# A 4-column addition between the exponentials' sums and their reciprocals, on GpSimd or on VectorE as a planner chooses

## Chip, cores and metric

The kernel runs on one core of a Trainium2 chip. The metric is the device time of one execution in microseconds, the median of several; smaller is better.

## The reference

Three blocks follow each other: an attention with a narrow causal window and some global keys, and two gated projections. In short:

```python
def _attn_ref(q, k, v, n_global, n_local):          # (2, 8, 768, 64)
    scores = scale * q @ k.T + bias                  # bias = -slope[h] * distance
    scores = where(keep, scores, -1e9)               # keep: k < 8, or 0 <= q - k < 96
    scores = scores - max(scores)
    a = np.exp(scores)
    a = a / (np.sum(a, axis=-1, keepdims=True) + 1e-09)
    return a @ v

def reference(...):
    x = attn_out.transpose(0, 2, 1, 3).reshape(2, 768, 512)
    x = (sigmoid(conv5(x)) * (x @ w_val)) @ w_out            # causal, per channel
    h = relu(x @ w_in)                                        # 512 -> 1024
    return (h * sigmoid(conv3(h))) @ w_out2                   # 1024 -> 512
```

The `1e-09` that is added to the sum of the exponentials is what the change is about.

## The kernel before

Attention works on 12 tiles (2 batches of 6 times 128 queries). A tile needs only its own and the previous 128 keys (256 columns); the global keys are copied over the first columns of the previous tile's (line 545, GpSimd). For each of two halves (4 heads) of a tile:

- TensorE makes the scores (line 492, PSUM tiles `s`).
- For each head VectorE adds mask and bias and takes the least value (line 503), and ScalarE takes the exponential and its sum (line 508). The sums of 4 heads lie beside each other in `st.t[:, 1]`, 128 rows by 4 columns.
- The *guard* (line 519) adds 1e-9 to these 4 columns, VectorE takes their reciprocal (line 522), and each head's probabilities `p` are multiplied by it: the *normalisation*, on VectorE (line 529), GpSimd (line 532) or ScalarE (line 535).

Then TensorE turns two heads' probabilities at a time (transposes, line 562, into the only PSUM bank `t`), ScalarE (line 566) or VectorE (line 572) copies them to `pts`, TensorE multiplies with the values (line 587, PSUM tile `x`), and a copy (line 604 or 610) puts the tile into `x`.

Beside that the weights are prepared: loads of 512 KB into three buffers `raw`, a conversion to fp32 by ScalarE, GpSimd and VectorE (lines 272 to 282), the product of `w_out` and `w_in` on TensorE (line 337, in 8 parts through two PSUM banks `f`) and its split into a high part by ScalarE (`Wh`, line 244) and a low part by VectorE (`Wl`, line 246). The projections follow per batch and half sequence: first tap (line 700 or 701), further taps on VectorE (line 705), tanh (line 707), and matmuls in three passes of high and low parts (lines 253 to 255).

No order is written by hand. Every piece of work is given to a `Plan` with an engine, an expected duration, and what it reads and writes. `Plan.add` takes one engine (and more as keywords); `Plan.any` takes a table of ways. `lay` builds a list schedule, backward for the ranks and forward for the order, in 6 passes, and `issue` keeps the pass with the earliest expected end. Where a piece has several ways, it goes where it is expected to end first:

```python
def here(w, e):
    ends = {o: max(free[o], est[w]) + us for o, (us, _) in w.ways.items()}
    return back or min(ends, key=ends.get) == e
```

All engines then run their instructions strictly in the planned order, and each waits for what its next instruction needs. So one changed duration or choice can move any work on any engine.

Of the kernel before, what the change touches and what calls it, by code (L numbers as in the profile page):

```python
# [14 lines left out]
ALU = mybir.AluOpType  # L15
# [205 lines left out]
def act_us(n, sbuf=True, scaled=False, sums=False):  # L221
    return 0.05 + 0.000834 * n + 0.042 * sbuf + 0.092 * scaled + 0.093 * sums


def dve_us(n, scaled=False):
    return 0.069 + 0.001042 * n + 0.061 * scaled
# [209 lines left out]
def fast_attention(c, ap):  # L436

    nc, ident, pl = c.nc, c.ident, c.plan
# [13 lines left out]
    def keys(t, pr, what):  # L452
        return key_tile(t)[:, pr, what]
# [18 lines left out]
    def held(d, ts):  # L472
        return [d[t] for t in ts if t in d]

    for t in range(nt):
        b, i = tiles[t]
        if t and i == 0:
            yield
        js = [t - 1, t] if i else [t]
        nk = len(js) * P  # L480
        st, p = sts.new(), {}
        load(t)
        for half in range(2):
            s = [c.ring["s"].new() for z in range(2)]

            def scores(half=half, s=s, js=js, t0=t):
                for pr in (2 * half, 2 * half + 1):
                    for n, j in enumerate(js):
                        for z in range(2):
                            hs = slice(z * D, (z + 1) * D)  # L490
                            out = s[z].t.rearrange("p (a w) -> p a w", w=WIN)[:, pr % 2, n * P : (n + 1) * P]
                            nc.tensor.matmul(out, keys(t0, pr, 1)[hs], keys(j, pr, 0)[hs], start=True, stop=True)  # L492

            pl.add(
                "PE", 0.43 * len(js), scores, s + held(kq, js), [("kq", j) for j in js], [("s", t, half)], mode="s"
            )
            for h in range(4 * half, 4 * half + 4):
                p[h] = pr_.new()

                def least(h=h, s=s, st=st, w=p[h], nk=nk, i=i):  # L500
                    sc = s[h % 2].t.rearrange("p (a w) -> p a w", w=WIN)[:, h // 2 % 2, :nk]
                    bias = c.B[:, h, :] if i else c.B0[h]
                    nc.vector.tensor_tensor_reduce(  # L503
                        w.t[:, :nk], sc, bias, -QKSCALE, 3.0e38, ALU.add, ALU.min, st.t[:, 0, h : h + 1]
                    )

                def grow(h=h, st=st, w=p[h], nk=nk):
                    nc.scalar.activation(  # L508
                        w.t[:, :nk], w.t[:, :nk], AF.Exp, bias=st.t[:, 0, h : h + 1], scale=-1.0,
                        accum_out=st.t[:, 1, h : h + 1],  # L510
                    )

                bias = ("B" if i else "B0", h)
                pl.add("DVE", dve_us(nk), least, [p[h], s[h % 2], st], [("s", t, half), bias], [("p", t, h)])
                pl.add("ACT", act_us(nk, True, True, True), grow, [p[h], st], [], [("p", t, h)])
            hs = slice(4 * half, 4 * half + 4)

            def guard(st=st, hs=hs):
                nc.gpsimd.tensor_scalar(st.t[:, 1, hs], st.t[:, 1, hs], 1.0e-9, 1.0, ALU.add, ALU.mult)

            def invert(st=st, hs=hs):
                nc.vector.reciprocal(st.t[:, 2, hs], st.t[:, 1, hs])  # L522

            four = [("p", t, h) for h in range(4 * half, 4 * half + 4)]
            pl.add("POOL", 0.12, guard, [st], four, [("r", t, half)])
            pl.add("DVE", 0.2, invert, [st], [], [("r", t, half)])
            for h in range(4 * half, 4 * half + 4):
                def on_dve(h=h, st=st, w=p[h], nk=nk):
                    nc.vector.tensor_scalar(w.t[:, :nk], w.t[:, :nk], st.t[:, 2, h : h + 1], None, ALU.mult)

                def on_pool(h=h, st=st, w=p[h], nk=nk):
                    nc.gpsimd.tensor_scalar(w.t[:, :nk], w.t[:, :nk], st.t[:, 2, h : h + 1], 1.0, ALU.mult, ALU.mult)  # L532

                def on_act(h=h, st=st, w=p[h], nk=nk):
                    nc.scalar.activation(w.t[:, :nk], w.t[:, :nk], AF.Copy, scale=st.t[:, 2, h : h + 1])

                pl.add(
                    "DVE", 0.22 + 0.00052 * nk, on_dve, [p[h], st], [("r", t, half)], [("p", t, h)],
                    POOL=(0.2 + pool_us(nk), on_pool), ACT=(act_us(nk, True, True), on_act),
                )  # L540

        def first_keys(t=t, i=i):
            r = key_tile(t)[:, :, 0, 0:GW]
            a, z = (gl, r) if i == 0 else (r, gl)
            nc.gpsimd.tensor_scalar(a, z, 1.0, 1.0, ALU.mult, ALU.mult)

        if i == 0:
            pl.add("POOL", 0.4, first_keys, held(kq, [t]), [("kq", t)], ["gl"])
        elif i < NT - 1:
            pl.add("POOL", 0.4, first_keys, held(kq, [t]), ["gl"], [("kq", t)])  # L550

        xp = c.ring["x"].new()
        pts = {}
        for pr in range(NPAIR):
            pt = c.ring["t"].new()
            pts[pr] = ptr.new()

            def turn(pr=pr, pt=pt, p=p, nw=len(js)):
                o = pt.t.rearrange("p (z n q) -> p z n q", z=2, n=2)
                for z in range(2):  # L560
                    for n in range(nw):
                        nc.tensor.transpose(o[:, z, n, :], p[2 * pr + z].t[:, n * P : (n + 1) * P], ident)  # L562

            def copy(pt=pt, w=pts[pr], nw=len(js)):
                o = pt.t.rearrange("p (z n q) -> p z n q", z=2, n=2)
                nc.scalar.activation(w.t[:, :, :nw, :], o[:, :, :nw, :], AF.Copy)  # L566

            two = [p[2 * pr], p[2 * pr + 1]]
            pl.add("PE", 0.218 * len(js), turn, [pt] + two, [("p", t, 2 * pr), ("p", t, 2 * pr + 1)], [("pt", t, pr)])
            def by_dve(pt=pt, w=pts[pr], nw=len(js)):  # L570
                o = pt.t.rearrange("p (z n q) -> p z n q", z=2, n=2)
                nc.vector.tensor_copy(w.t[:, :, :nw, :], o[:, :, :nw, :])

            pl.add(
                "ACT", act_us(2 * nk, False), copy, [pt, pts[pr]], [("pt", t, pr)], [("pts", t, pr)],
                DVE=(dve_us(2 * nk), by_dve),
            )

            if pr % XPAIRS < XPAIRS - 1:
                continue  # L580

            def output(prs=range(pr - XPAIRS + 1, pr + 1), pts=pts, xp=xp, js=js):
                o = xp.t.rearrange("p (a q) -> p a q", q=P)
                for pr in prs:
                    for n, j in enumerate(js):
                        for z in range(2):
                            nc.tensor.matmul(  # L587
                                o[z * D : (z + 1) * D, pr, :], vals(j, 2 * pr + z), pts[pr].t[:, z, n, :],
                                start=n == 0, stop=n == len(js) - 1,
                            )  # L590

            prs = range(pr - XPAIRS + 1, pr + 1)
            pl.add(
                "PE", 0.213 * len(js) * XPAIRS, output, [xp] + [pts[q] for q in prs] + held(vs, js),
                [("pts", t, q) for q in prs] + [("v", j) for j in js], [("xp", t, q) for q in prs], mode="x",
            )
        if 0 < i < NT - 1:
            pl.add(
                "SP", dma_us(64), lambda b=b, t=t: nc.sync.dma_start(vs[t].t[0:GW], c.v[b, 0:GW].rearrange("s (a h) d -> s a h d", a=2)),
                [vs[t]], [], [("v", t)], delay=LANDING,  # L600
            )
        pl.add(
            "ACT", act_us(512, False),
            lambda xp=xp, i=i: nc.scalar.activation(
                c.x[:, :, XP + i * P : XP + (i + 1) * P], xp.t.rearrange("p (a q) -> p a q", q=P), AF.Copy
            ),
            [xp], [("xp", t, pr) for pr in range(NPAIR)], [("x", i)] + (["d", "d0"] if t in (0, 1, 4) else []),
            DVE=(
                dve_us(512),
                lambda xp=xp, i=i: nc.vector.tensor_copy(  # L610
                    c.x[:, :, XP + i * P : XP + (i + 1) * P], xp.t.rearrange("p (a q) -> p a q", q=P)
                ),
            ),
        )
# [431 lines left out]
```

## Time and profile before

| | us |
|---|---|
| median of 3 runs | 285.17 (284.56 to 285.33) |
| profiled execution, its own time | 285.38 |
| its span, first to last instruction | 283.2 |
| TensorE busy | 269.5 |
| VectorE busy | 233.6 |
| ScalarE busy | 196.8 |
| GpSimd busy | 86.1 |

Busy shares are averages over stages with different limits, so the windows tell more than the sum. A wait is put down to what ended it last. A busy TensorE is not TensorE at its peak, since the end of a matmul is modelled: where it matters, read the distance from one start to the next. In the rows PE is TensorE, PEld its weight load, DVE VectorE, ACT ScalarE, POOL GpSimd; `t<-ident,p` means that tile `t` is written from `ident` and `p`. TensorE's granted clock is 0.997 of full speed over the span.

### The profile page before, as it was taken

What the parts mean: (1) busy time and instruction counts of PE and PEld (TensorE: products, weight loads), DVE (VectorE), ACT (ScalarE), POOL (GpSimd) and SP (SyncE); (2) the same over time, 40 slices, a digit from 0 to 9 for tenths busy, and PEclk for the clock granted to TensorE, in tenths of its full rate; (3) what the DMA queues carried; (4) which work ended last, traced back from release to release, by engine and by line L of the source; (5) the groups of instructions that cost most, each with busy time, mean ns of one, the idle gap of its engine ahead of it and who ended that gap; (6) DMA issues with size and microseconds to landing.
All of it is one profiled execution on the core that took longest, in us unless ns stands there. A gap on an engine that the chain in (4) does not pass through costs nothing.

```text
span 283.2 us, 5424 instructions
## 1 busy us (share of the span) xinstructions
PE 269.5 (95%) x1832; PEld 227.8 (80%) x1832; DVE 233.6 (83%) x587; ACT 196.8 (69%) x501; POOL 86.1 (30%) x194
## 2 busy tenths in 40 slices
PE   3898899999999999999999999999999999999993
PEld 2676765664449999999999999889999988899882
DVE  3999999999999999998999999999985653357600
ACT  2999999979799998887588356773673354544520
POOL 4645447645136124363244330050202000002000
PEclk9999999999999999999999999999999999999998
DMA  5986748556443701004200000010000011000021
GB/s 160 346 298 211 236 149 313 169 176 222 152 117 117 263 0 49 9 2 148 88 0 0 3 0 0 0 39 38 37 2 0 0 74 39 37 1 2 38 111 49
DMA packets 10420, 26.17 MB, mean 92 GB/s; under 512 B 1424, under 2 KB 2704, under 8 KB 10384
## 3 DMA queue, kind: packets, MB, share of 16 engines
q1 hardware_dynamic: 9968, 25.22, 26.4%
q10 hardware_dynamic: 416, 0.52, 0.5%
q8 instruction: 16, 0.26, 0.4%
q14 instruction: 20, 0.16, 0.2%
HBM read 22.59 MB, written 3.15 MB: 91 GB/s over the span
## 4 chain that ended last, share of the span: by engine, by line
PE 71%; DVE 13%; ACT 6%; issue 5%; POOL 2%; DVEq 1%; POOLq 0%; ACTq 0%
PE s L254 8%; PE s L255 8%; PE s L253 8%; PE f L253 8%; PE f L254 7%; PE f L255 7%; PE s L492 4%; PE t L562 4%; PE x L587 3%; DVE z L705 3%; ACT p L508 3%; DVE p L503 3%; PE t L255 2%; PE x L255 2%; PE t L254 2%
## 5 line engine op out<-in xcount | busy, mean ns | idle before, releaser
L705 DVE SCALAR_TENSOR_TENSOR z<-h,cw,z 128x384 f32<-128x384 f32 x64 | 40.2, 635 | 13.5 <-ACT z L700 11.6
L508 ACT ACTIVATE p<-p,st 128x256 f32<-128x256 f32 (+1 forms) x96 | 46.0, 482 | 2.2 <-DVE st L503 0.8
L707 ACT ACTIVATE z<-z 128x384 f32<-128x384 f32 (+2 forms) x48 | 24.9, 523 | 24.9 <-DVE z L705 24.6
L705 DVE SCALAR_TENSOR_TENSOR z<-x,cw,z 128x400 f32<-128x400 f32 (+1 forms) x64 | 39.8, 657 | 0.1
L254 PE MATMUL s<-w,g 128*128 128x512 f32 (+1 forms) x104 | 39.2, 377 | 0.0
L255 PE MATMUL s<-w,g 128*128 128x512 f32 (+1 forms) x104 | 39.2, 377 | 0.0
L253 PE MATMUL s<-w,g 128*128 128x512 f32 (+1 forms) x104 | 39.1, 376 | 0.0
L562 PEld LDWEIGHTS t<-ident,p 128*128 128x128 f32 x176 | 20.1, 141 | 15.7 <-ACT pts L566 5.7
L562 PE MATMUL t<-ident,p 128*128 128x128 f32 x176 | 28.8, 283 | 2.9 <-ACT pts L566 2.2
L337 PE MATMUL f<-w,w 128*128 128x512 f32 x64 | 30.9, 602 | 0.6 <-DVE Wl L246 0.6
L503 DVE CUSTOM_DVE_ANT_0 p<-s,B 128x256 f32<-128x256 f32 x80 | 30.4, 413 | 0.0
L253 PE MATMUL f<-gg,Wh 128*128 128x400 f32 (+1 forms) x80 | 27.7, 346 | 0.0
L254 PE MATMUL f<-gg,Wh 128*128 128x400 f32 (+1 forms) x80 | 27.1, 339 | 0.0
L255 PE MATMUL f<-gg,Wl 128*128 128x400 f32 (+1 forms) x80 | 27.0, 338 | 0.0
L532 POOL TENSOR_SCALAR p<-p,st 128x256 f32<-128x256 f32 (+1 forms) x34 | 21.4, 634 | 18.4 <-DVE st L522 16.2
L274 POOL TENSOR_SCALAR raw<-raw 128x512 f32<-128x512 f32 x24 | 18.7, 781 | 21.2 <-ACT m L272 14.9
L246 DVE TENSOR_TENSOR g<-z,g 128x384 fp32r<-128x384 f32 x32 | 18.0, 572 | 5.9 <-ACT g L244 5.9
L255 PEld LDWEIGHTS s<-w,g 128*128 128x128 f32 x104 | 19.5, 188 | 4.0 <-DVE g L246 0.2
L253 PEld LDWEIGHTS s<-w,g 128*128 128x128 f32 x104 | 19.5, 188 | 2.8
L254 PEld LDWEIGHTS s<-w,g 128*128 128x128 f32 x104 | 19.5, 188 | 2.7
L818 DVE SCALAR_TENSOR_TENSOR z<-z,h 128x384 f32<-128x384 f32 x32 | 18.3, 577 | 4.1 <-ACT z L707 3.6
L587 PE MATMUL x<-pts,v 128*64 128x128 f32 x320 | 21.2, 277 | 0.0
(126 smaller groups left out, 656.3 us busy)
## 6 DMA issues: line engine op xcount, KB each, us to landing
raw<-in_moe_w_out_dram SPq DMA_DIRECT2D x12, 512.0 KB, 3.4
raw<-in_moe_w_in_dram SPq DMA_DIRECT2D x8, 512.0 KB, 4.3
k<-in_kq_dram SPq DMA_DIRECT2D x7, 512.0 KB, 4.9
v<-in_v_dram SPq DMA_DIRECT2D x11, 256.0 KB, 4.2
out_dram<-o SPq DMA_DIRECT2D x11, 256.0 KB, 2.0
raw<-in_moe_w_val_dram SPq DMA_DIRECT2D x4, 512.0 KB, 3.6
kq<-in_kq_dram SPq DMA_DIRECT2D x3, 512.0 KB, 4.8
v<-in_v_dram SPq DMA_DIRECT2D x8, 64.0 KB, 2.8
```

The lines of the kernel that those rows point to most:

```text
L253: nc.tensor.matmul(out, lh, rh, start=first, stop=False)
L254: nc.tensor.matmul(out, lh, rl, start=False, stop=False)
L255: nc.tensor.matmul(out, ll, rh, start=False, stop=last)
L274: "POOL", pool_us(n), lambda: nc.gpsimd.tensor_scalar(whole(), whole(), 0.0, 1.0, ALU.mult, ALU.mult),
L337: nc.tensor.matmul(ps.t, big["wot"].t.bitcast(F32)[:, e, cs], big[wi].t.bitcast(F32)[:, e, :], start=e == 0, stop=e == 3)
L503: nc.vector.tensor_tensor_reduce(w.t[:, :nk], sc, bias, -QKSCALE, 3.0e38, ALU.add, ALU.min, st.t[:, 0, h : h + 1])
L508: nc.scalar.activation(w.t[:, :nk], w.t[:, :nk], AF.Exp, bias=st.t[:, 0, h : h + 1], scale=-1.0, accum_out=st.t[:, 1, h : h + 1],)
L532: nc.gpsimd.tensor_scalar(w.t[:, :nk], w.t[:, :nk], st.t[:, 2, h : h + 1], 1.0, ALU.mult, ALU.mult)
L562: nc.tensor.transpose(o[:, z, n, :], p[2 * pr + z].t[:, n * P : (n + 1) * P], ident)
L587: nc.tensor.matmul(o[z * D : (z + 1) * D, pr, :], vals(j, 2 * pr + z), pts[pr].t[:, z, n, :], start=n == 0, stop=n == len(js) - 1,)
L705: nc.vector.scalar_tensor_tensor(z(), src(k), w()[:, k : k + 1], z(), ALU.mult, ALU.add)
L707: pl.add("ACT", act_us(n), lambda: nc.scalar.activation(z(), z(), AF.Tanh, scale=0.5), bufs, [], [token])
```

## The change

The guard, which GpSimd alone did, gets a second way on VectorE, and its expected duration on GpSimd is raised from 0.12 to 0.3 us (0.16 on VectorE).

```diff
             def guard(st=st, hs=hs):
                 nc.gpsimd.tensor_scalar(st.t[:, 1, hs], st.t[:, 1, hs], 1.0e-9, 1.0, ALU.add, ALU.mult)
 
+            def dguard(st=st, hs=hs):
+                nc.vector.tensor_scalar(st.t[:, 1, hs], st.t[:, 1, hs], 1.0e-9, None, ALU.add)
+
             def invert(st=st, hs=hs):
                 nc.vector.reciprocal(st.t[:, 2, hs], st.t[:, 1, hs])
 
             four = [("p", t, h) for h in range(4 * half, 4 * half + 4)]
-            pl.add("POOL", 0.12, guard, [st], four, [("r", t, half)])
+            pl.any({"POOL": (0.3, guard), "DVE": (0.16, dguard)}, [st], four, [("r", t, half)])
             pl.add("DVE", 0.2, invert, [st], [], [("r", t, half)])
```

The planner then lays out everything anew: most rows of every engine's order stand elsewhere. Lines behind the edit have numbers 3 higher in the changed kernel. Of the 24 guards 5 stand on VectorE there: those of the first half of the first three tiles, and both of the eleventh.

Of the 96 normalisations 27 stood on VectorE, 34 on GpSimd and 35 on ScalarE; now 31, 41 and 24 do.

VectorE at the first tile, before: the row behind the mask's distance (line 418), with the first reciprocal (`st` is the tile of least values, sums and reciprocals, `b` and `B` the masks).

```order
L418 TENSOR_SCALAR x<-x,li 128x32
L503 ISA p,st<-s,b_234 128x128
L503 ISA st 128x1
L522 RECIPROCAL st<-st 128x4
L401 TENSOR_SCALAR B<-x 128x256
L529 TENSOR_SCALAR p<-p,st 128x128 x2
```

And now:

```order
L418 TENSOR_SCALAR x<-x,li 128x32
L522 TENSOR_SCALAR st<-st 128x4
L525 RECIPROCAL st<-st 128x4
L503 ISA p,st<-s,b_234 128x128
L503 ISA st 128x1
L401 TENSOR_SCALAR B<-x 128x256
L532 TENSOR_SCALAR p<-p,st 128x128 x2
```

The guard stands on VectorE, with its reciprocal directly behind it, and the score reduction that stood ahead comes after.

TensorE from the eleventh group of transposes on (26.42 us in the trace before), before (`x8` are two groups of four):

```order
L562 MATMUL t<-ident,p 128x128 x8
L492 MATMUL s<-kq,k_71 128x128 x2
L492 MATMUL s<-k_71 128x128 x2
L492 MATMUL s<-kq,k_71 128x128 x2
L492 MATMUL s<-k_71 128x128 x2
L587 MATMUL x<-pts,v_73 64x128 x2
```

And now:

```order
L565 MATMUL t<-ident,p 128x128 x4
L590 MATMUL x<-pts,v_73 64x128 x2
L590 MATMUL x<-pts,v 64x128 x2
L590 MATMUL x<-pts,v_73 64x128 x2
L590 MATMUL x<-pts,v 64x128 x2
L565 MATMUL t<-ident,p 128x128 x4
L492 MATMUL s<-kq,k_71 128x128 x2
```

An output group has moved in between the two groups of transposes; it stood behind the scores that follow them.

VectorE at the sixth lower part of the product weights (`Wl`; about 77 us in the trace before), before. It is row 244 of VectorE's order, with equal neighbours counted as one row:

```order
L503 ISA st 128x1
L705 SCALAR_TENSOR_TENSOR z<-x,cw,z 128x400
L246 TENSOR_TENSOR wvl<-m,wvh 128x512
L503 ISA p,st<-s,B 128x256
L503 ISA st 128x1
L246 TENSOR_TENSOR Wl<-f,Wh 128x512
L279 SCALAR_TENSOR_TENSOR raw_76<-raw_76 128x512
```

And now, where it is row 216:

```order
L503 ISA p,st<-s,B 128x256
L503 ISA st 128x1
L246 TENSOR_TENSOR wvl<-m,wvh 128x512
L246 TENSOR_TENSOR Wl<-f,Wh 128x512
L525 RECIPROCAL st<-st 128x4
```

Ahead of it fewer score reductions, taps and copies stand than before.

## Rows read from the trace of the kernel before

**Rows 1.** Busy time of each engine, page part 1: us (share) xinstructions

```profile
PE 269.5 (95%) x1832; PEld 227.8 (80%) x1832; DVE 233.6 (83%) x587; ACT 196.8 (69%) x501; POOL 86.1 (30%) x194
```

**Rows 2.** Windows (us), length; busy us of PE, PEld, DVE, ACT, POOL; clock; DMA

```profile
20.00:30.00 10.00, 8.79 (x106) 7.00 (x105) 9.89 (x39) 10.00 (x32) 4.42 (x11) 1.00 0.52 169
...
140.00:160.00 20.00, 20.00 (x122) 18.65 (x118) 19.87 (x36) 14.64 (x31) 8.32 (x15) 1.00 0.01 1
```

**Rows 3.** TensorE's waits, by releaser: us in total, times, longest

```profile
PE s L492 <- DMA x<-in_kq_dram: 4.8, 1, 4.8
PE t L562 <- ACT pts L566: 2.2, 4, 1.2
```

**Rows 4.** Timelines, 25 to 36 us, TensorE and then ScalarE: start, us, what

```profile
26.42 0.66 PE L562 MATMUL t<-ident,p 128*128 128x128 f32 x4
28.29 0.65 PE L562 MATMUL t<-ident,p 128*128 128x128 f32 x4 [1.21 <-ACT pts L566]
...
31.86 0.66 PE L562 MATMUL t<-ident,p 128*128 128x128 f32 x4
33.20 0.66 PE L562 MATMUL t<-ident,p 128*128 128x128 f32 x4 [0.69 <-ACT pts L566]
...
31.43 0.51 ACT L508 ACTIVATE p<-p,st 128x256 f32<-128x256 f32 x1 [0.67 <-POOL k L545]
```

**Rows 5.** Timeline of TensorE, 60 to 84 us

```profile
63.07 1.02 PE L337 MATMUL f<-w,w 128*128 128x512 f32 x2
64.25 0.44 PE L562 MATMUL t<-ident,p 128*128 128x128 f32 x2 [0.15 <-ACT pts L566]
...
75.41 1.88 PE L337 MATMUL f<-w,w 128*128 128x512 f32 x4
77.94 2.84 PE L337 MATMUL f<-w,w 128*128 128x512 f32 x6 [0.65 <-DVE Wl L246]
...
81.74 1.12 PE L337 MATMUL f<-w,w 128*128 128x512 f32 x2
83.02 0.66 PE L562 MATMUL t<-ident,p 128*128 128x128 f32 x4 [0.16 <-ACT pts L566]
83.52 1.02 PE L337 MATMUL f<-w,w 128*128 128x512 f32 x2
```

**Rows 6.** Lines 519 and 522: duration in ns min/median/max, first and last start

```profile
L519 POOL TENSOR_SCALAR st<-st x24: 192/196/675, 8.3 to 122.9; 128x4 f32<-128x4 f32 x24
...
L522 DVE RECIPROCAL st<-st x24: 159/171/178, 8.8 to 123.6; 128x4 f32<-128x4 f32 x24
```

**Rows 7.** Chain that ended last: start, us on the chain, engine and line

```profile
34.70 0.48 ACT pts L566
...
37.31 0.40 ACT p L535
...
41.57 0.27 DVE p L529
...
51.38 0.60 DVE pts L572
...
62.52 0.34 DVE p L503
62.87 0.55 DVE z L705
...
64.02 0.60 DVE Wl L246
...
83.68 0.86 PE f L337 x2
...
106.45 1.09 PE s L492 x16
```

**Rows 8.** Line 532, normalisation on GpSimd: durations, and who waited for it

```profile
L532 POOL TENSOR_SCALAR p<-p,st x34: 369/490/1615, 9.3 to 123.9; 128x256 f32<-128x256 f32 x26, 128x128 f32<-128x128 f32 x8
...
  PEld t L562: 0.3, 1
```

## The prediction

> **What bounds the kernel now.** I read the busy times first, then the windows, then what TensorE waited for, then its timeline at each wait. TensorE is busy for 269.5 of 283.2 us [rows 1]. The windows say where the rest lies: of the ten microseconds from 20 it is busy 8.79, while VectorE and ScalarE are busy 9.89 and 10.00; of the twenty from 140 it is busy all 20 [rows 2]. So the attention part at the start runs at the pace of VectorE and ScalarE, and later TensorE alone sets the pace. Its work is the same before and after, so the end moves by what it loses while it waits, and by nothing else. What VectorE, ScalarE or GpSimd save is worth nothing unless it ends such a wait.
>
> The list of its waits is short: 4.8 us for the first keys, then 2.2 us in four waits for copies out of PSUM by ScalarE [rows 3]; each other releaser makes under 1 us. These idle times are too small, because a matmul's end is modelled. Distances from start to start tell the loss better. Four transposes take 0.50 us (83.02 to 83.52), and a pair of weight products 0.86 us [rows 5, 7]. Then the losses are: 28.29 − 26.42 − 0.50 = 1.37 and 33.20 − 31.86 − 0.50 = 0.84 [rows 4]; 64.25 − 63.07 − 0.86 = 0.32, 77.94 − 75.41 − 1.72 = 0.81 and 83.02 − 81.74 − 0.86 = 0.42 [rows 5]. Together 3.8 us: 2.2 early, 1.55 late. The rest of the listed idle time lies in the first tiles, before 18 us.
>
> **The guard itself.** Two lines change, but the planner lays the whole program anew. By the orders 5 of the 24 guards go to VectorE, 19 stay. GpSimd loses 5 x 0.196 = 1.0 us [rows 6]. The trace has no add of 4 columns on VectorE. The nearest row is the reciprocal of the same shape behind it, 0.171 us [rows 6]; the farther one is a copy of 512 columns, 0.60 us [rows 7]. I take 0.17, so 5 x 0.17 = 0.85 us more on VectorE, with bounds of 0 (it may lie wholly under its neighbours) and 3.0 us. What waits behind a guard there is VectorE's queue: it stands until the fourth exponential is done. That costs little, because the reciprocal behind it in the same queue waits for the same exponentials already, through GpSimd. And what the guards took on GpSimd lay beside other work: it is busy for 30% of the span [rows 1].
>
> [...]
>
> **The new order.** The new price of a guard on GpSimd (0.3 for 0.12) and the choice move much else: normalisations go from 35 ScalarE, 34 GpSimd, 27 VectorE to 24, 41 and 31; VectorE gives seven copies out of PSUM to ScalarE (net). ScalarE sheds 11 x 0.40 = 4.4 us and takes five copies of 0.48 and two half as wide, 2.9; GpSimd takes 7 x 0.49 = 3.4 [rows 7, 8]. None of that moves the end by itself. I therefore look at each wait of TensorE and count, in the two orders, what stands ahead of it.
>
> At 77.94 TensorE waits for the sixth lower part of the product weights (Wl), since the products have two PSUM banks. In VectorE's order there stand ahead of that split 9 fewer score reductions (9 x 0.34 = 3.1), 5 fewer convolution taps (5 x 0.55 = 2.7), 5 fewer PSUM copies (two of 0.60, three narrow ones of about 0.34: 2.2), one pair fewer of weight conversions of 512 columns (2 x 0.60 = 1.2); and more: three splits net (1.3), two mask rows (0.6), two normalisations (2 x 0.27 = 0.5) [rows 7] (estimates by columns from the nearest row where a shape has none). The three added guards replace three reciprocals. Sum: −6.8 us. TensorE has 2 score groups, 4 transpose groups and 1 output group fewer ahead: 2 x 1.09 + 4 x 0.50 + 1.09 = 5.3 us [rows 5, 7] (the output group at a score group's price, which has as many matmuls). So the split comes 6.8 us sooner where TensorE comes 5.3 sooner: 1.5 us gained where 0.81 were lacking. That wait goes, and about 0.7 us of room stands there.
>
> At 83.02 ten normalisations fewer (4.0 us) stand ahead on ScalarE, and TensorE has 4 us more ahead (a score group of 1.09, a weight product of 0.86, and the first value product); 0.42 us goes. At 64.25 TensorE has 14 more products ahead (14 x 0.86 = 12.0, about 11 net of other groups), while ScalarE has 1.3 us more and VectorE 10; the room grows by some 0.9 us where 0.32 were lacking. What is late next at these places is VectorE, with somewhat under 1 us of room by the same count.
>
> The early two stay. Ahead of the transposes at 33.20 ScalarE has four copies more (three of 0.48, one of half the width) and two normalisations of 0.40 and a mask row of about 0.3 fewer: 1.7 − 1.1, about +0.6 us [rows 7]; against that, an idle 0.67 us of ScalarE at 31.43 [rows 4], where its exponential needs a score reduction of VectorE, should close, because that reduction stands earlier in VectorE's order. At 28.29 an output group is drawn ahead, which fills part of the wait and leaves a like one in front of itself. I put the stretch before 35 us at 0, between −2.2 (both waits gone) and +0.8.
>
> TensorE goes from scores or outputs to other work 36 times in place of 35 by the orders; I cost one such step at nothing.
>
> Sum: −0.32 − 0.81 − 0.42 + 0 = −1.55 us. The profiled execution took 285.38 us, 283.2 of them span; that makes 283.8. The median of the runs is 285.17, 0.2 below, and gives 283.6. I predict **283.7**.
>
> **Rivals.** *The front takes it back.* If ScalarE's +0.6 us and the four extra copies (each bank of turned probabilities waits for its copy) delay the early turns by 0.8 us, −1.55 + 0.8 gives 285.17 − 0.75 = 284.4, within the noise. For it: ScalarE has no idle time between 20 and 30 us [rows 2]. Against it: the extra is 0.6 us, and the idle time ahead of it, 0.67 us [rows 4], is as long.
>
> *GpSimd becomes late (slower).* 41 normalisations in place of 34 run on it, and each is followed by a transpose on TensorE. They take 369 to 1615 ns about a median of 490 [rows 8], so a stretched one is 1.1 us late. Two of them in front of TensorE already undo the gain; three give 285.17 − 1.55 + 3 x 1.13 = 287.0. It decides when TensorE's waits for GpSimd pass 2.4 us. Against it: with 34 of them TensorE's weight loads waited 0.3 us, once [rows 8], and the work ahead of its turns leaves over 1 us nearly everywhere. [...]
>
> *The edit is what it says and no more.* If the new order is as good as the old one, only five guards count: between 0 and 0.85 us of VectorE in a stretch where it is busy 9.89 of 10 [rows 2], so 285.2 to 286.0, and most likely the former.
>
> **How the numbers follow.** About 0.3% (0.86 us) is what a measurement of this kernel can tell from no change. Forecast 0.52; front takes it back 0.25; no more than the edit 0.08; GpSimd late 0.15. Faster 0.52, the same 0.32, slower 0.16 (the slow case and a little of the third). The range goes down to 281.4 (285.17 − 1.55 − 2.2: the early waits gone too) and up to 286.4, which takes in the second and third cases and the lesser half of the slow one.
>
> **What would show it.** In the profile after, TensorE's waits should list ScalarE copies near 28 and 33 us and no wait for Wl; the waits at 64, 78 and 83 us should be gone, and from there on its windows should be full. VectorE stays near 233 us, ScalarE falls by 1.5 us or more (4.4 − 2.9) from 196.8, GpSimd rises by 2 to 5 from 86.1 [rows 1]. Wrong would be: a wait of over 0.5 us for a GpSimd normalisation; new waits of TensorE after 40 us, perhaps behind ScalarE standing for a weight load at line 272, since the conversions are drawn together; or a gain that comes from the first 35 us.

## The result, and the profile after

The changed kernel takes 288.76 us (288.62 to 289.46, 4 runs); the kernel before took 285.11 beside it. The ratio is 1.0133 (95% interval 1.0118 to 1.0147): slower by 3.65 us, where 283.7 was predicted. The profiled execution took 289.46 us, 287.6 of them span, 4.4 more than before.

Page part 1 of the profile after answers to [rows 1]:

```profile
PE 271.5 (94%) x1832; PEld 229.1 (80%) x1832; DVE 233.5 (81%) x591; ACT 193.8 (67%) x492; POOL 94.4 (33%) x199
```

VectorE is where it was, ScalarE has 3.0 us less, GpSimd 8.3 more, and 1832 matmuls stand in either profile. So the time went into what TensorE lost while it waited or ran slower. Its list of waits, by line and releaser (us in total, times, longest; four of its six rows), answers to [rows 3]:

```profile
PE s L492 <- DMA x<-in_kq_dram: 4.8, 1, 4.8
PE x L590 <- DMA v<-in_v_dram: 2.6, 1, 2.6
PE t L565 <- DVE pts L575: 1.3, 3, 0.5
PE t L565 <- ACT pts L569: 0.9, 2, 0.7
```

The second row is new: an output group (line 590) stood 2.6 us for a load of values. TensorE's timeline after, 26 to 37 us (start, us, what, idle time before it), answers to [rows 4]:

```profile
26.85 0.66 PE L565 MATMUL t<-ident,p 128*128 128x128 f32 x4
30.07 1.09 PE L590 MATMUL x<-pts,v 128*64 128x128 f32 x16 [2.56 <-DMA v<-in_v_dram]
31.09 1.04 PE L565 MATMUL t<-ident,p 128*128 128x128 f32 x4
32.07 0.80 PE L492 MATMUL s<-kq,k 64*128 64x128 f32 x4
...
34.08 1.34 PE L590 MATMUL x<-pts,v 128*64 128x128 f32 x16
...
36.69 0.66 PE L565 MATMUL t<-ident,p 128*128 128x128 f32 x4 [0.69 <-ACT pts L569]
```

This is the place where the prediction said that an output group is drawn ahead. Before, transposes stood at 28.29, waiting for a copy, and the output groups of tile 2 came behind them and the scores:

```profile
29.96 1.97 PE L587 MATMUL x<-pts,v 128*64 128x128 f32 x32
```

Now the first output group of tile 2 stands ahead of those transposes. It reads tile 1's values, whose first 32 rows had just been replaced by the global ones: a load of 64 KB (line 599, after the edit 602), which SyncE issues when tile 1's own outputs are done. SyncE's timeline, before and then after (start, us to issue, what is loaded):

```profile
23.06 0.33 SPq L467 DMA_DIRECT2D k<-in_kq_dram  x1
24.85 0.34 SPq L599 DMA_DIRECT2D v<-in_v_dram  x1
25.64 0.35 SPq L309 DMA_DIRECT2D raw<-in_moe_w_out_dram  x1
```

```profile
23.50 0.33 SPq L467 DMA_DIRECT2D k<-in_kq_dram  x1
25.15 0.33 SPq L309 DMA_DIRECT2D raw<-in_moe_w_out_dram  x1
25.57 0.38 SPq L602 DMA_DIRECT2D v<-in_v_dram  x1
```

The 64 KB now stand behind a 512 KB weight load. The view of the line, over the stretch that holds this load (599 before, then 602 after), gives the time to landing:

```profile
DMA to landing us min/median/max: 2.2/2.2/2.2
```

```profile
DMA to landing us min/median/max: 4.4/4.4/4.4
```

So the values landed near 27.1 before and near 29.9 after, 0.17 us behind the large load (29.93 and 29.76). The words "All engines then run ... in the planned order" ahead of the prediction were too wide: that holds for the four engines that compute (line 45 names them). SyncE's order is made outside the plan, and there it came out the other way.

What followed the wait cost time too. Windows of the profile after (stretch, length, busy us of PE, PEld, DVE, ACT, POOL, granted clock, DMA share, GB/s):

```profile
30.00:31.00 1.00, 0.93 (x16) 0.88 (x16) 0.00 (x0) 1.00 (x3) 0.99 (x2) 1.00 0.44 94
31.00:32.00 1.00, 1.00 (x8) 0.64 (x4) 0.00 (x0) 0.72 (x4) 0.13 (x1) 0.61 0.97 381
32.00:33.00 1.00, 1.00 (x9) 0.93 (x10) 0.82 (x2) 0.00 (x0) 0.00 (x0) 0.50 0.19 66
33.00:34.00 1.00, 1.00 (x12) 0.85 (x8) 1.00 (x7) 0.60 (x2) 0.00 (x0) 0.50 0.00 0
34.00:35.00 1.00, 1.00 (x14) 0.92 (x14) 0.90 (x4) 0.00 (x0) 0.68 (x2) 0.69 0.34 49
```

The clock fell to 0.50 behind the 2.56 us in which TensorE stood idle, and was back at 1.00 by 35 us. In the first window after the wait it was still 1.00. VectorE and ScalarE, which set the pace there, stand idle in turn: VectorE waits 2.27 us for the transposes, ScalarE 1.60 us for the scores and 1.54 us for an output group.

After 60 us, four waits of TensorE are listed (timeline):

```profile
76.69 1.98 PE L337 MATMUL f<-w,w 128*128 128x512 f32 x4 [0.30 <-DVE Wl L246]
...
80.16 0.41 PE L565 MATMUL t<-ident,p 128*128 128x128 f32 x2 [0.41 <-DVE pts L575]
...
120.24 0.63 PE L565 MATMUL t<-ident,p 128*128 128x128 f32 x4 [0.40 <-DVE pts L575]
...
137.60 0.66 PE L565 MATMUL t<-ident,p 128*128 128x128 f32 x4 [0.17 <-ACT pts L569]
```

Those at 64 and 83 us [rows 5] are gone, the one for Wl is smaller (0.65 to 0.30), and three others have come.

For sums I count as the prediction does, over all matmuls: from each start to the next, less what the first takes when nothing is in its way (estimates from the distances of starts in the trace of before: 55 ns in scores, 52 in outputs, 109 in transposes, 429 in weight products, 0.453 ns for a column elsewhere, where 512 columns have medians of 231 to 236). Lost by TensorE, in us:

| | to 40 us | 40 to 50 | 50 to 150 |
|---|---|---|---|
| before | 12.9 | 1.0 | 8.05 |
| after | 15.85 | 0.2 | 9.9 |

With the stretch behind TensorE's last start, 5.1 us before and 5.5 after, that is the 4.4 us of span. The idle time listed after 60 us grew by 0.3 us only (0.96 to 1.28); the rest of the 1.85 us in the last column is smaller losses, which weren't taken apart.

### The profile page after: what moved, and what is told of

The parts are those of the page before. It is cut to its first block, busy times and chain, and to the rows that moved or that the text cites. A ratio compares the mean times of both kernels' runs of the same rounds, so it can differ in the third digit from the quotient of the medians.

```text
span 287.6 us, 5437 instructions
## 1 busy us (share of the span) xinstructions
PE 271.5 (94%) x1832; PEld 229.1 (80%) x1832; DVE 233.5 (81%) x591; ACT 193.8 (67%) x492; POOL 94.4 (33%) x199
## 4 chain that ended last, share of the span: by engine, by line
PE 67%; DVE 23%; ACT 3%; issue 3%; DMA 2%; DVEq 1%; POOL 0%; ACTq 0%; POOLq 0%
PE s L254 8%; PE s L255 8%; PE s L253 8%; DVE z L708 7%; PE s L492 5%; PE f L255 5%; PE f L253 5%; PE f L254 5%; DVE p L503 4%; PE x L590 4%; PE t L565 4%; PE f L337 3%; PE t L253 2%; DVE raw L279 2%; PE x L255 2%
## 5 line engine op out<-in xcount | busy, mean ns | idle before, releaser
L708 DVE SCALAR_TENSOR_TENSOR z<-h,cw,z 128x384 f32<-128x384 f32 x64 | 40.8, 643 | 12.8 <-ACT z L703 11.6
L704 POOL TENSOR_SCALAR z<-h,cw 128x384 f32<-128x384 f32 x11 | 11.8, 1077 | 57.4 <-DVE z L708 31.0
L535 POOL TENSOR_SCALAR p<-p,st 128x256 f32<-128x256 f32 (+1 forms) x41 | 22.8, 561 | 14.3 <-DVE st L525 8.8
L590 PEld LDWEIGHTS x<-pts,v 128*64 128x64 f32 x320 | 17.6, 138 | 6.9 <-issue 2.9
L255 PEld LDWEIGHTS s<-w,g 128*128 128x128 f32 x104 | 19.5, 188 | 3.9
L569 ACT ACTIVATE pts<-t 128x512 f32<-128x512 f32 (+1 forms) x36 | 20.3, 565 | 2.5 <-PE t L565 2.3
```

Source lines behind the costliest of these rows:

```text
L255: nc.tensor.matmul(out, ll, rh, start=False, stop=last)
L590: nc.tensor.matmul(o[z * D : (z + 1) * D, pr, :], vals(j, 2 * pr + z), pts[pr].t[:, z, n, :], start=n == 0, stop=n == len(js) - 1,)
L708: nc.vector.scalar_tensor_tensor(z(), src(k), w()[:, k : k + 1], z(), ALU.mult, ALU.add)
```

## Experiments: the load and the place of the output group

Theory A: the loss is the wait for the late values, with the clock behind it. Theory B: the new plan as a whole is worse, and the wait only stands where another would. All comparisons are with the kernel before on the same chip (284.8 to 284.9 us).

**The load put first.** Step 102 of the plan is the values' load, step 302 the weight load ahead of it (in the diffs `...` marks lines left out):

```diff
-            w.ways[w.eng][1]()
+            go(w, laid)
...
+def go(w, laid):
+    if laid and w.n == 302:
+        with TC["tc"].issue_after(TC[102].ins):
+            w.ways[w.eng][1]()
+    else:
+        TC[w.n] = w.ways[w.eng][1]()
```

> The changed kernel, with one edit: on SyncE's queue the 64 KB load of the global values for tile 2 (line 602) stands ahead of the 512 KB weight load that the changed kernel issues just before it; TensorE, VectorE, ScalarE and GpSimd have the changed kernel's rows. Theory A, the late load: the load now lands near 27.5 us instead of 29.93, TensorE's wait for it falls from 2.6 us to under 0.4, the granted clock stays at full speed in 31 to 35 us (it lost about 1.7 us there), and the time falls by 3.5 to 4.3 us from 288.8 to 284.5 to 285.3. Theory B, the plan as a whole (later waits at 60, 76, 79, 104, 120 and 137 us and the slower GpSimd carry the loss, and the early wait only stands where another would have stood): 287.5 or more.

Measured: 285.62 us, ratio 1.0038 (1.0018 to 1.0057). TensorE's waits and its timeline there:

```profile
PE x L590 <- DMA v<-in_v_dram: 0.8, 1, 0.8
```

```profile
27.79 1.09 PE L590 MATMUL x<-pts,v 128*64 128x128 f32 x16 [0.75 <-DMA v<-in_v_dram]
```

One load's place on SyncE takes away 2.8 of the 3.65 us (2.4 of 3.2 by the repeated run of the changed kernel further down), less than theory A said; the wait is 0.8, not under 0.4, and the clock stays at 1.00 from 30 to 37 us. 0.9 us stay. Theory B's 287.5 did not come.

**The output group put back.** With `move`, one step is taken out of the order and put ahead of or behind another:

```diff
-            self.finish(order)
+            self.finish(order), move(order)
...
+MOVES = [(141, 211, 1)]
...
```

> The changed kernel, with one edit on TensorE: the first output group of tile 2 goes back behind the two transposes groups and the scores of the next tile, where the kernel before has it (on SyncE two later loads of values also change places); the 512 KB load stays ahead of the values. Theory A: the load still lands near 29.9 us, but nothing asks for it before about 30, the wait for it is under 0.5 us, the clock does not fall, 284.8 to 286. Theory B: 287.5 or more.

Measured: 285.66 us, 1.0031 (1.0019 to 1.0044). The load again stands behind the large one, no wait for it is listed, and the group starts at 29.73 behind transposes and scores:

```profile
28.05 0.66 PE L565 MATMUL t<-ident,p 128*128 128x128 f32 x4 [0.85 <-ACT pts L569]
...
29.73 1.97 PE L590 MATMUL x<-pts,v 128*64 128x128 f32 x32
```

So most of the loss needs both halves, the late load and the group ahead. Taking either away gives the same 285.6.

**The kernel before, with the group ahead** (`MOVES = [(141, 144, 0)]`).

> The kernel before, with one edit on TensorE: the first output group of tile 2 ahead of the second transposes group, as the changed kernel has it; the values' load stays ahead of the 512 KB load and lands at 27.06 us. Theory A: no new wait for a load, the time stays within 0.5 us of 285.1. Theory C, the place of the output group itself costs (it waits for ScalarE's or VectorE's copies and holds up the transposes): 286.5 or more.

Measured: 286.88 us, 1.0069 (1.0051 to 1.0087): slower by 2.1, which is in theory C's range and not in theory A's. The load was in time (issued at 24.3, 2.2 us to landing), and another releaser stood there:

```profile
28.69 1.18 PE L587 MATMUL x<-pts,v 128*64 128x128 f32 x16 [2.18 <-ACT x L604]
```

The group waits for ScalarE's copy of tile 1 out of the same PSUM tile, which in the order of before stands late on ScalarE. So the group's new place costs time without the order of ScalarE that belongs to it.

**The kernel before, with both** (group ahead, and the 512 KB load ahead of the values).

```diff
+MOVES = [(141, 144, 0), (302, 297, 1), (102, 302, 1)]
...
+    if laid and w.n == 102:
+        with TC["tc"].issue_after(TC[302].ins):
...
```

> The kernel before, with two edits: the first output group of tile 2 ahead of the second transposes group, and the 512 KB weight load ahead of the 64 KB load of values on SyncE. No guard is moved and nothing else of the plan. Theory A: this alone makes the whole loss: the load lands near 29.9 us, TensorE waits for it over 2 us, the granted clock falls to half speed behind that wait, 288 to 289.3. Theory B: at most 286.

Measured: 287.57 us, 1.0106 (1.0088 to 1.0124), 0.4 us under theory A's range, with this row in the timeline of the profiled execution, whose clock stays at 1.00 from 30 to 37 us:

```profile
29.40 1.09 PE L587 MATMUL x<-pts,v 128*64 128x128 f32 x16 [2.46 <-DMA v<-in_v_dram]
```

The wait is made again, in a plan in which no guard was moved. But the copy of the run before would have held the group nearly as long, so this one alone doesn't separate the causes.

## Experiments: clock, guard, price and choice

**TensorE kept at work through the wait.**

```diff
+                for _ in range(FILL if js == [1, 2] and prs[0] == 0 else 0): nc.tensor.transpose(o[:, 0, :], ident, ident)
...
+FILL = 20
```

> The changed kernel, and 20 transposes of the identity into the output group's own bank (overwritten right after) ahead of the group that waits 2.6 us, so that TensorE works through that wait; 20 at 0.11 us are 2.2 us. Theory A2, the clock has its own part in the loss and falls because TensorE stood idle: the wait stays (the load lands near 29.9 us as before), the granted clock stays at full speed in 31 to 35 us, and the time falls by 0.7 us (from the four executions of the run with both edits: 286.83 us at a mean clock of 0.999, 288.24 at 0.989, so 0.14 us for a thousandth, and the changed kernel has 0.993) to 1.7 us (its rows between 31 and 35 us): 287.1 to 288.1. Rival: the clock falls for another reason or costs nothing at the end: 288.4 or more.

Measured: 288.16 us, 1.0126 (1.0104 to 1.0148), between the two ranges. The clock is 1.00 from 29 to 36 us, but the filling itself ends at 30.3, after the load has landed (no wait for it is listed). With 14 transposes:

> The changed kernel with 14 instead of 20 transposes of the identity ahead of the output group, so that they end before the load lands and only the clock is changed. If the fall of the clock has its own share, as the choice-only kernel's executions say (median 285.95 at 0.997 to 1.0, 287.88 at 0.992 to 0.994): 1 to 2 us under the changed kernel on the same chip. If the loss is the wait alone: within 0.5 us of it.

Measured: 287.96 us, 1.0095 (1.0068 to 1.0121). In its profile the clock is at 1.00 from 29 to 36 us, but 0.51 at 14 to 16 us, so an execution's mean clock doesn't tell where it fell. Beside it on the same chip the changed kernel once more:

> The changed kernel once more, unaltered, so that it stands beside the others on one chip: 288.2 to 289, a wait for the values of 2 to 2.8 us, mean clock 0.991 to 0.994.

Measured: 288.02 us (287.07 to 289.76), 1.0115 (1.0083 to 1.0148). The filling gained nothing that can be told: 287.96 is within 0.5 us of it, as expected for a loss that is the wait alone, but the executions of either kernel spread over more than 2 us, and the expected 1 to 2 us compare with executions that have the fall. The repeated kernel, though, shows the price of the clock: in its profiled execution (287.57 us) the same wait left the clock alone. Its timeline, and two of its windows:

```profile
29.87 1.09 PE L590 MATMUL x<-pts,v 128*64 128x128 f32 x16 [2.17 <-DMA v<-in_v_dram]
...
34.94 0.66 PE L565 MATMUL t<-ident,p 128*128 128x128 f32 x4 [0.69 <-ACT pts L569]
```

```profile
32.00:33.00 1.00, 1.00 (x20) 0.88 (x19) 1.00 (x5) 0.27 (x1) 0.26 (x1) 1.00 0.28 102
33.00:34.00 1.00, 1.00 (x18) 0.83 (x12) 1.00 (x4) 0.62 (x3) 0.23 (x2) 1.00 0.47 98
```

From the output group to the same transposes it is 34.94 − 29.87 = 5.07 us here and 36.69 − 30.07 = 6.62 in the first profile: 1.55 us for the fall of the clock, in an execution that has it. In both, TensorE resumed at a clock of 1.00; in the first profile the clock was at half from 1.1 us later (31.2 us, by the 0.61 of that window), in the other it stayed at 1.00. Of the ten executions of the changed kernel, seven have a mean clock of 0.991 to 0.994 and took 288.31 to 289.76 us (median 288.84); three have 0.998 or 0.999 and took 287.07 to 287.72 (median 287.57). These 1.3 us fit the 1.55, but only a profiled execution tells where its clock fell. So in the medians, and in the 2.8 us, a part is likely the clock's; its size, and that the idle time is what makes the clock fall, weren't shown.

**The five guards alone**, in the plan of before:

```diff
+                e = nc.vector if (t, half) in ON_DVE else nc.gpsimd
+                e.tensor_scalar(st.t[:, 1, hs], st.t[:, 1, hs], 1.0e-9, 1.0, ALU.add, ALU.mult)
...
+ON_DVE = [(0, 0), (1, 0), (2, 0), (10, 0), (10, 1)]
```

> The kernel before with its plan kept as it is, and only the five guards that the changed kernel moved (first halves of tiles 0, 1 and 2, both halves of tile 10) done by VectorE at the same place in the order. Theory A: the moved guard itself costs or gains nothing that can be told, 284.7 to 285.6. Rival: the guard on VectorE holds up the scores' minima behind it and is part of the loss: 286 or more; or it gains what the prediction hoped for: under 284.2.

Measured: 284.89 us, 0.9999 (0.9987 to 1.0011). Moving these guards by itself costs and gains nothing that can be told.

**The price alone** (0.12 to 0.30, all guards on GpSimd), and **the choice alone** (0.12 kept):

```diff
-            pl.add("POOL", 0.12, guard, [st], four, [("r", t, half)])
+            pl.add("POOL", 0.3, guard, [st], four, [("r", t, half)])
```

> The kernel before with one number: the guard's price on GpSimd in the plan 0.30 instead of 0.12; all 24 guards stay on GpSimd, and the plan is laid again. It again puts the 512 KB load ahead of the 64 KB load of values, and the first output group of tile 2 ahead of the next scores, but behind both transposes groups. Theory A: a wait for the values of 0.5 to 2 us, 285.5 to 287.5. Theory B, the higher price in itself spoils the plan: 288 or more. Theory D, the choice of engine was what hurt and the price does no harm: at most 285.2.

Measured: 286.13 us, 1.0044 (1.0029 to 1.0059), within theory A's range, with 0.4 us of wait for the values (0.5 to 2 expected) and 1.1 for a copy of ScalarE ahead of it.

```diff
-            pl.any({"POOL": (0.3, guard), "DVE": (0.16, dguard)}, [st], four, [("r", t, half)])
+            pl.any({"POOL": (0.12, guard), "DVE": (0.16, dguard)}, [st], four, [("r", t, half)])
```

> The changed kernel with one number: the guard's price on GpSimd 0.12, as the kernel before has it, instead of 0.30; the choice between the engines stays (7 of 24 guards go to VectorE). The plan is laid again; in its first 30 us SyncE's queue and TensorE's order read as in the changed kernel: the 512 KB load ahead of the values, the output group ahead of the second transposes group. Theory A: the same wait of 2 to 2.8 us and the same loss, 287.5 to 289.5. Theory B, the higher price is what did the harm: at most 286.

Measured: 286.24 us (285.29 to 288.22), 1.0055 (1.0027 to 1.0083), between the two theories. The wait is there, shorter:

```profile
29.01 1.09 PE L590 MATMUL x<-pts,v 128*64 128x128 f32 x16 [1.50 <-DMA v<-in_v_dram]
```

The same kernel with the load put first, as in the first experiment:

> The plan of the choice-only kernel (guard's price on GpSimd 0.12, the choice kept), and on SyncE the 64 KB load of values ahead of the 512 KB load. Theory A: the wait for the values (1.5 us in its profiled execution, more in those whose mean clock is 0.992 to 0.994 and which end near 287.9) goes, no execution is left near 288, and the median falls by 1 to 2 us from 286.2 to 284.2 to 285.2. Theory B, the new plan's later waits set the time: 286 or more.

Measured: 284.87 us, 1.0009 (0.9989 to 1.0029). The load's place is worth 1.4 us here, and this is the only plan with the choice that isn't slower than the kernel before. None beat it.

**SyncE in the order of the plan**, changed kernel:

```diff
-ORDERED = {getattr(mybir.EngineType, e) for e in ("PE", "DVE", "Activation", "Pool")}
+ORDERED = {getattr(mybir.EngineType, e) for e in ("PE", "DVE", "Activation", "Pool", "SP")}
```

> The changed kernel, but SyncE's queue follows the plan's order like the other engines', instead of being ordered by itself; the 64 KB load then stands ahead of the weight load, and a good many later loads change places. Theory A: no wait of over 0.8 us for values, 284.8 to 286.5. Rival: the plan's order of loads makes TensorE or the conversions wait elsewhere, 287 or more.

Measured: 286.14 us, 1.0038 (1.0023 to 1.0053). No wait for values is listed: in the plan the small load does stand first. Other loads moved too; the ratio is that of the single move (1.0038 in both), so what they did can't be told.

## Experiments: the later plan

After the load was put right 0.9 us stayed. The order was therefore written out as a list, the first 280 of 1404 steps from one plan and the rest from the other:

```diff
-            self.finish(order)
+            take(order)
...
+def take(order):
+    of = {w.n: w for w in order}
+    order[:] = [of[int(x[:-1])] for x in ORDER.split()]
+    for x in ORDER.split():
+        of[int(x[:-1])].eng = ENGS[x[-1]]
```

> The two plans spliced: the first 280 of 1404 steps (TensorE to about 42 us) in the changed kernel's order with its engines (three of its five moved guards among them), the rest in the order of the kernel before. SyncE's queue has the 512 KB load ahead of the values, as in the changed kernel. Theory A+ (the wait for the values carries some 2.8 us of the loss and the later plan the remaining 0.9): 287 to 288 (before 284.8), with the wait of 2 to 2.6 us. If the front carries all: over 288. If the front carries little: under 286.3.

Measured: 288.64 us, 1.0130 (1.0104 to 1.0156). By itself this would say that the front carries all; the sums below show a seam in it. Its five executions go from 286.83 us (mean clock 0.997, the profiled one) to 289.08 (0.991). In the profiled one the output group stood 1.85 us, less than expected; the list puts that down to ScalarE (line 508), but the values, issued at 25.2, had landed near 28.8 (3.6 us to landing), only about 0.2 us before the group started (29.00).

> The opposite splice: the first 280 steps in the order of the kernel before, the rest in the changed kernel's order with its engines (the two guards of tile 10 on VectorE). No wait for the values. Theory A+: 0.5 to 1.3 us over the kernel before, 285.3 to 286.1, with waits near 59, 72, 75, 116 and 133 us. If the later plan gains what was predicted (1.5 us) and only the front takes it back: under 284.

Measured: 286.87 us, 1.0069 (1.0049 to 1.0088). That is more than expected; its timeline has the later waits of the changed kernel again, each 2.6 us earlier than there, and ahead of them one that neither plan has, at the seam:

```profile
57.91 1.12 PE L337 MATMUL f<-w,w 128*128 128x512 f32 x2 [0.76 <-DVE w L282]
74.11 1.98 PE L337 MATMUL f<-w,w 128*128 128x512 f32 x4 [0.30 <-DVE Wl L246]
77.58 0.41 PE L565 MATMUL t<-ident,p 128*128 128x128 f32 x2 [0.41 <-DVE pts L575]
117.68 0.63 PE L565 MATMUL t<-ident,p 128*128 128x128 f32 x4 [0.42 <-DVE pts L575]
```

> The first splice (front of the changed kernel, rest of the kernel before), and the 64 KB load of values ahead of the 512 KB load on SyncE. Theory A+: the wait for the values under 0.8 us, and the front, which in the kernel with that one edit lost 12.5 us of TensorE's time up to 50 us against 13.8 in the kernel before, now gains: 283.5 to 284.8, perhaps under both kernels. If the front of the new plan is no better once the load is in time: 284.8 to 285.5.

Measured: 286.00 us, 1.0035 (1.0019 to 1.0052), above the expected range.

TensorE's loss in the profiled executions, counted as above:

| | to 40 us | 40 to 50 | 50 to 150 |
|---|---|---|---|
| load put first | 12.2 | 0.3 | 9.65 |
| front of changed, rest of before | 13.4 | 2.1 | 8.15 |
| front of before, rest of changed | 12.5 | 0.5 | 10.4 |
| front of changed with load first, rest of before | 12.5 | 2.2 | 8.0 |

The last column goes with the later plan: 8.0 to 8.15 for that of before (before itself 8.05), 9.65 to 10.4 for the changed one, 0.7 of the 10.4 at the seam. So the later plan loses some 1.6 us more. With the load put first the sum closes: 0.7 us less to 40 us, 0.7 less to 50, 1.6 more to 150 and 0.4 more behind TensorE's last start make 0.6 us of span (283.8 against 283.2), and the 0.9 us that stay are such a balance. The seam (two waits for ScalarE's copies, 0.69 us at 46 and 0.64 at 50 us) costs the other splice about 1.1 us; by these sums that is why the third one isn't under both kernels. The new front with its load in time loses 0.4 to 0.7 us less up to 40 us than before. Which steps of the later plan make its new waits wasn't taken apart further.

## Why the prediction was wrong

- *What bounds the kernel* held: the end moved with what TensorE lost. Its lost time grew by 4.1 us, its span by 4.4.
- *The guard itself* held. It takes 0.161 us on VectorE (five in 0.8 us; predicted 0.17), and moving the five alone changes nothing (0.9999).
- *"The early two stay ... I put the stretch before 35 us at 0"* is the first of two steps that failed, and it made most of the slowdown. The prediction saw the output group drawn ahead at 28 us and asked only which engine's copy it would wait for. It left out the transfer: which load the group reads, where that stands on SyncE, and when it lands. In the trace of before the load landed at 27.06 and was wanted at 29.96, so it showed in no list of waits. By the first two experiments this is worth 2.8 of the 3.65 us, against an upper bound of 0.8 in the text. A smaller matter: the prediction laid ScalarE's idle 0.67 us at 31.43 to a score reduction of VectorE, while the row names GpSimd's copy of the global keys [rows 4]; the reduction ended 0.1 us earlier, so the row doesn't decide.
- *The waits at 64, 78 and 83 us, −1.55* is the second, and failed as a sum. The first and the last went as counted. That for Wl shrank by half where 0.7 us of room was claimed. And others came, for VectorE's copies at 80 and 120 us: the prediction named VectorE as next in line, but counted what stands ahead of three waits that existed and gave nothing for places where none had been. From 50 to 150 us TensorE lost 1.85 us more, not 1.55 less. Against the forecast these 3.4 us are the larger error: up to 50 us, late load and slow clock included, it lost 2.15 more where 0 was put. Which step of the later plan opens the new waits stays open; the splices show only that they go with that plan.
- *The rivals.* GpSimd did not become the bound: only weight loads waited for a normalisation on it, 0.5 us in two places, and one transpose 0.6 us for a mask that GpSimd makes (line 399, at 12 us), though it is busy 8.3 us more, against a predicted 2 to 5 (22 first taps of the projections stand there in place of 19, and take 4.8 us more). Nor did its normalisations get longer: 41 took 367 to 962 ns with a median of 479, where 34 had taken 369 to 1615 with 490. *The edit is what it says and no more*, 285.2 to 286.0, is what is left once the load is in time (285.6), but by luck: the guards cost nothing, and the 0.9 us are a gain early and a larger loss later. *The front takes it back* had the right place, but put 0.8 us on ScalarE's copies. No rival had the transfer, so the range ended at 286.4.

## What to carry to other kernels

Where a planner moves work ahead, follow every input of the moved work to its producer, transfers included, and ask when they land and not only whether they were waited for before; a queue whose order the plan does not make has to be read as it comes out. A plan that is laid again is a new plan: all three that were laid anew here cost 0.4 to 1.3% although the edit itself cost nothing, so count places where new waits can open, not just the old ones that close.

## What the runs showed of the hardware

- A 64 KB load landed 2.2 us after its issue in the kernel before, with and without the group ahead, and 2.8 us after it in the changed kernel with the load put first: there it stood ahead of the 512 KB load. Behind that load it landed 4.4 us after its issue in the changed kernel, 0.17 us after the large one, and 3.6 us after it with the front of the changed kernel alone.
- The granted clock fell to 0.50 behind an idle time of TensorE of 2.56 us in one execution of the changed kernel, and behind 2.18 us in the kernel before with the group ahead (0.50 to 0.51 from 30 to 33 us). It stayed at 1.00 behind 2.17 us in another execution of the changed kernel, and behind 2.46 us in the kernel before with both edits.
- The guards left on GpSimd became longer: 24 took 6.9 us before (mean 286 ns), 19 took 8.7 after (mean 458 ns). Why wasn't tried; no wait for one of them is listed after.
